# Infini-attention and SwiGLU, two layers on one core: K's masked odd copy on a compute engine, corner masks in halves, and a new hand-written order

## The chip, the cores and the metric

One core of a Trainium2 chip runs the whole program; the metric is its time on the device in microseconds. TensorE multiplies into PSUM, ScalarE and VectorE read PSUM and write SBUF, GpSimd works in SBUF alone, and SyncE issues most of the DMAs. In rows of a profile the engines are PE (PEld: its weight loads), ACT, DVE, POOL and SP.

## The reference

Two layers of the same two blocks over 2048 tokens of width 512. `_A_ref` has 32 heads of width 16 and goes through the sequence in four segments of 512 tokens: softmax attention inside a segment, mixed by a gate with a read of a memory M that the earlier segments have filled. `_B_ref` is a gated feed-forward block of width 1376.

```python
for s in range(N):                                  # 4 segments of L = 512
    logits = jnp.einsum('bhqd,bhkd->bhqk', qs, ks) * scale + mask
    p = _softmax(logits, axis=-1)
    a_dot = jnp.einsum('bhqk,bhkd->bhqd', p, vs)
    ...
    o = g * a_mem + (1.0 - g) * a_dot
    M = M + jnp.einsum('bhld,bhle->bhde', pk, vs)
...
x = x + _A_ref(_layernorm(x, axis=-1), A_wq, A_wk, A_wv, A_wo, A_beta)
x = x + _B_ref(_layernorm(x, axis=-1), B_w1, B_w3, B_w2)   # and both once more
```

The mask is causal: a query sees the keys up to its own place in its segment.

## The kernel before

The work is cut into eight passes g = 0 to 7 (two layers of four segments). A pass has a layer norm, the projections to Q, K and V (`project`), attention in units (`attention`), the memory's update and read, the output projection, a second layer norm and the feed-forward block (`ffn`). Passes overlap: while the attention of g runs, TensorE also has the feed-forward matmuls of g - 1 and the projections of g + 1.

**Attention units.** `unit_list` cuts a pass into units of up to 512 columns for four heads at a time, 18 in a pass (pass 0 runs in two parts). Of each unit TensorE writes the logits (operations R, line 983) into PSUM, ScalarE writes their exponential to a tile `e` (line 999), GpSimd zeroes what the causal mask hides in it (line 1008, `affine_select`), and two units later TensorE multiplies by V (operations C, line 1054). A unit of kind "f" holds blocks of keys by queries, with a mask of 4 x 64 elements a partition for each block on the diagonal. A unit of kind "s" holds the shared corners: 32 blocks of 64 columns, masked by two instructions of 2048 elements a partition, one on 64 partitions and, behind it, one on 128. There are 16 such units.

**K's masked copies.** The heads lie 16 rows apart, and a matmul takes 32 rows. For the heads with an odd number the kernel keeps a copy of K in which the even rows are zero (tile `km`, its "odd" columns, `kodd`), for the corners a second one in which the odd rows are zero ("even" columns, `kev`, operation ke). In passes 0 and 1 the odd copy is a VectorE multiplication of K by a column of zeros and ones (`cm[1]`, line 795). From pass 2 on the zeros already stand in the two buffers of `km`, and four DMAs of 64 KB, on GpSimd's queue, copy only the odd rows of K (line 803): 24 DMAs in all. Logits of odd heads and of corners wait for them.

**The order.** The operations are built in program order, and then issued in an order written out by hand: `ORDER` lists all 3699 operations by number, over all engines at once; each engine takes its own in that order, and buffers are handed out along it. `OTHER` lists the operations that have two possible engines and take the second one: evacuations of PSUM (`ev`, line 519 on VectorE and 518 on ScalarE), ke, and some steps of the normalisation. Waits between engines are semaphores. One rule is added in `schedule`: an operation of GpSimd waits for all VectorE operations of the kinds in `SHARED` that stand ahead of it in the order. Names that the prediction uses: norm (line 689), vj (a shifted copy of V, line 785), phmin (line 832), evv, evk, evq, evt (evacuations of V, K, Q and of the transposed input), macc (line 862, an addition to the memory).

```python
SHARED = ("vj", "ke", "norm", "lnve", "t", "rdg", "ph", "phmin", "mblk", "km", "oadd")
            ...
            if e == "dve" and op.group[0] in SHARED:
                handed.append(op)
            elif e == "pool" and op.dmaq is None:
                for d in handed:
                    op.deps[d.seq] = d
                handed = []
```

Of the kernel before, what the change touches and what calls it, by code (L numbers as in the profile page):

```python
# [3 lines left out]
ACT = mybir.ActivationFunctionType  # L4
# [4 lines left out]
P = 128  # L9
# [3 lines left out]
NCG = 4  # L13
# [239 lines left out]
def o_pe(ns):  # L253
# [7 lines left out]
    0 9 30 23 29 32 2-3 31 34 33 35 5 10 4 21 1 11-12 36-37 13-16 6 17 44 38-39 45-46 18-19 40 47-48 20 41 55 43 22  # L261
    49-53 56 42 57 78-79 102 8 80 90-91 103 92 81 85 68 54 86-88 82 7 67 58-59 69 60 83 104-107 61 108 89 84 27 64
    93-94 109-110 186 188 97-99 113-114 100 115-116 111 95 187 117-118 24 189 119-120 191 112 96 101 200 673 201 70
    121 671 62-63 74-75 667 65 674 66 71 25 127-128 194 196 190 129 672 134-136 668 193 137-138 669-670 675-676
    139-140 154-155 195 208 141-142 130 197-198 224 122 72-73 192 209 199 225 156-157 145 131 146 123-124 147 158
    125 210 365 226 211 215 214 680 159-160 212 165 148 143 677 126 179 166 227 231 149-150 161 213 133 202-204 366
    683 151-152 167-169 162 180 229 153 132 174 368 170 230 256 258 175 181 228 216 369 163 257 686 144 171-172 259
    367 164 173 371 176 264 177 358 217 265 207 178 240 266 182 267 684 241 260 248 261 685 183 274 76 206 269 268
    678-679 275 744 205 272-273 270 218 271 687 745 681 276 249 277 262 184 746 370 284 185 232 688 682 263 1112
    705 242 747 77 285 28 722 282 233 283 250 748 243 280 706-708 281 26 709 1113 251 739-742 294 710 244-245 743  # L270
    278-279 286 689 723 252 254 296 295 724 246 297 300 700 1114-1115 298 253 1108 1110 701 372 219 308 299 287 725
    1109 220 304 1111 1116 309 726 234 305 690 247 702 691-692 703 306 302 704 301 235 373-374 310 1117 1119
    236-237 711 288 238 307 239 320 376 303 1122 328 1118 321 693 712 329 318 713 319 324 716 332 311 694 322 333
    1121 377 695 325-326 714-715 1120 323 378 756 327 1123 696-697 222 698 344 289 334 717 749 255 345 342-343 757
# [146 lines left out]
def build(nc, A_x, A_wq, A_wk, A_wv, A_wo, A_beta, B_w1, B_w3, B_w2, out):  # L421
# [530 lines left out]
    def attention(s, g, z, oms, parts):  # L952
        z.ot = new("W")
        cnt = 0
        for pi, part in enumerate(parts):
# [4 lines left out]
            for ui, (blocks, done, N) in enumerate(todo):  # L960
# [3 lines left out]
                for pgs in groups:  # L964
# [22 lines left out]
                    for (kind, G, ee, j, c, n) in blocks:  # L987
# [6 lines left out]
                        if kind == "s" or ee:  # L994
                            rd += [(z.km, G, j // 2)] if g <= 1 else [(z.km, pg, "p") for pg in pgs]
# [288 lines left out]
```

## Time and profile before

| | us |
|---|---|
| three runs of the kernel before | 495.35, 501.39, 504.0 |
| their median | 501.39 |
| the profiled execution, its own time | 496.81 |
| its span, first to last instruction | 495.1 |

The profile is of one execution, 4.6 us faster than the median of the three runs. Its time is 1.7 us more than its span. Times in rows are from the span's start. A row of the timeline gives start and duration, both in us, the engine, the line, the operation and its tiles; "x8" means that eight instructions in a row are merged into one, under the form of the first, and a bracket names how long the engine stood idle ahead of it and what ended that. PEclk is TensorE's granted clock as a share of 2.4 GHz.

### The profile page before, as it was taken

How to read it: one execution, taken by the hardware profiler on the slowest of the kernel's cores; microseconds unless marked ns; L12 is line 12 of the kernel's file. 1: busy time of each engine (PE TensorE's matmuls, PEld its weight loads, DVE VectorE, ACT ScalarE, POOL GpSimd, SP SyncE). 2: the span in 40 equal slices, each digit the busy share in tenths (PEclk: the TensorE clock that was granted, in tenths of full speed). 3: DMA queues.
4: the chain of work that ended last, by engine and by line, in shares of the span. 5: the costliest groups of instructions: out<-in, count | busy, mean ns of one | idle time of the engine just before them, and what ended most of it. 6: DMA issues, size and time to landing. Idle time of an engine off the chain costs nothing.

```text
span 495.1 us, 19697 instructions
## 1 busy us (share of the span) xinstructions
PE 470.1 (95%) x8808; PEld 241.0 (49%) x8808; DVE 401.2 (81%) x836; ACT 376.4 (76%) x359; POOL 251.2 (51%) x408
## 2 busy tenths in 40 slices
PE   7789989799999998999999999899999999999997
PEld 4444435576445443544444545354444544455554
DVE  7998899588699788788987888886796699689673
ACT  6687997589899997799988879779997887651130
POOL 4774276275538573556745554755474743540000
PEclk9888999799999999999999999999999999999999
DMA  7662427733522725443254613444224411441402
GB/s 242 242 98 50 83 56 138 117 78 71 72 45 56 98 34 97 65 69 68 33 93 57 98 27 66 59 72 87 44 34 72 50 39 28 80 75 54 99 1 77
DMA packets 106548, 37.49 MB, mean 76 GB/s; under 512 B 99200, under 2 KB 104448, under 8 KB 106464
## 3 DMA queue, kind: packets, MB, share of 16 engines
q1 hardware_dynamic: 104016, 31.41, 33.8%
q0 software_dynamic: 1488, 4.03, 5.1%
q8 instruction: 69, 1.13, 1.0%
q10 hardware_dynamic: 960, 0.79, 0.5%
q14 instruction: 15, 0.12, 0.1%
HBM read 8.43 MB, written 2.10 MB: 21 GB/s over the span
## 4 chain that ended last, share of the span: by engine, by line
PE 78%; DVE 12%; DMA 4%; issue 2%; ACT 2%; POOL 1%; SPq 0%; POOLq 0%
PE psall L233 32%; PE psall L228 30%; PE psall L983 8%; PE psall L1054 6%; DVE W L832 2%; DMA W<-xn 2%; ACT e L999 1%; DVE xn L689 1%; DMA x_tok<-in_A_x_dram 1%; DVE W L519 1%; DVE ln L670 1%; DVE km L795 1%; DVE vj L785 1%; POOL e L1008 1%; DMA xg<-xs 1%
## 5 line engine op out<-in xcount | busy, mean ns | idle before, releaser
L999 ACT ACTIVATE e<-psall 128x2048 bf16<-128x2048 f32 (+1 forms) x162 | 271.3, 1691 | 46.3 <-PE psall L983 44.3
L1008 POOL TENSOR_SCALAR_AFFINE_SELECT e<-e 128x256 bf16<-128x256 bf16 (+2 forms) x288 | 173.7, 627 | 135.3 <-ACT e L999 76.0
L228 PE MATMUL psall<-W,w 128*128 128x512 bf16 (+1 forms) x365 | 84.3, 360 | 1.5 <-DMA W<-xn 1.0
L233 PE MATMUL psall<-W,w 128*32 128x512 bf16 (+1 forms) x1420 | 82.2, 361 | 0.0
L1173 ACT ACTIVATE th<-psall 128x512 bf16<-128x512 f32 x80 | 47.1, 600 | 24.2 <-PE psall L233 21.4
L1179 DVE SCALAR_TENSOR_TENSOR h<-gp,psall 128x512 bf16<-128x512 bf16 x80 | 53.7, 679 | 11.8 <-PE psall L228 5.8
L1175 DVE SCALAR_TENSOR_TENSOR gp<-th,psall 128x512 bf16<-128x512 bf16 x80 | 53.8, 680 | 11.2 <-ACT th L1173 10.7
L233 PE MATMUL psall<-w,h 128*32 128x512 bf16 (+2 forms) x968 | 58.0, 370 | 1.3 <-DVE h L1179 1.3
L228 PEld LDWEIGHTS psall<-W,w 128*128 128x128 bf16 x365 | 33.8, 100 | 35.6 <-issue 3.8
L233 PEld LDWEIGHTS psall<-W,w 128*32 128x32 bf16 x1420 | 37.1, 97 | 27.1 <-issue 4.0
L670 DVE BATCH_NORM_STATS2 ln<-x_tok 128x6 f32<-128x512 bf16 x64 | 42.9, 679 | 1.6 <-DMA x_tok<-in_A_x_dram 1.2
L1091 POOL TENSOR_TENSOR og<-xg,rd 128x256 bf16<-128x256 bf16 (+1 forms) x46 | 27.7, 606 | 31.9 <-DVE rd L1085 12.6
L519 DVE CAST W<-psall 128x512 bf16<-128x512 f32 (+1 forms) x48 | 32.0, 677 | 9.8 <-PE psall L228 7.0
L1054 PE MATMUL psall<-e,va 128*32 128x192 bf16 (+4 forms) x1088 | 39.6, 266 | 0.1
L1198 DVE TENSOR_TENSOR x_tok<-psall,x_tok 128x512 bf16<-128x512 f32 (+1 forms) x33 | 22.0, 673 | 21.4 <-PE psall L233 13.1
L983 PE MATMUL psall<-W,km 32*128 32x64 bf16 (+4 forms) x1056 | 37.5, 230 | 0.0
L233 PEld LDWEIGHTS psall<-w,h 128*32 128x32 bf16 (+1 forms) x968 | 25.2, 96 | 21.3 <-issue 2.1
L1054 PE MATMUL psall<-e,vj 128*32 128x64 bf16 x1024 | 30.1, 194 | 4.2 <-issue 3.4
L228 PE MATMUL psall<-wv,W 128*128 128x512 bf16 x94 | 30.0, 397 | 4.0 <-DVE va L519 3.7
L228 PE MATMUL psall<-w,h 128*128 128x512 bf16 (+1 forms) x121 | 32.4, 380 | 0.0
L983 PE MATMUL psall<-W 16*128 16x64 bf16 (+4 forms) x544 | 31.4, 274 | 0.8 <-DVE W L519 0.6
L679 POOL TENSOR_TENSOR ln<-ln,mhalf 128x4 f32<-128x4 f32 (+1 forms) x17 | 16.8, 989 | 29.7 <-DVE ln L676 26.7
(98 smaller groups left out, 671.5 us busy)
## 6 DMA issues: line engine op xcount, KB each, us to landing
w<-in_B_w_dram SPq DMA_DIRECT2D x4, 688.0 KB, 8.5
out_dram<-x_tok SPq DMA_DIRECT2D x15, 128.0 KB, 1.8
km<-W POOLq DMA_DIRECT2D x24, 64.0 KB, 3.4
w<-in_B_w_dram POOLq DMA_DIRECT2D x3, 384.0 KB, 5.2
x_tok<-in_A_x_dram POOLq DMA_DIRECT2D x2, 512.0 KB, 8.8
xg<-xs SPq DMA_TRANSPOSE x36, 3.3
W<-og SPq DMA_TRANSPOSE x36, 2.6
wk<-in_A_wk_dram SPq DMA_DIRECT2D x1, 512.0 KB, 4.5
```

Source lines behind the costliest of these rows:

```text
L228: return e.matmul(out, lhsT, rhs, **k)
L233: o = e.matmul(out[c:c + 32], lhsT[:, c:c + 32], rhs, tile_position=(0, c), **k)
L519: return e.tensor_copy(dst(), src())
L670: dve(lambda e: e.bn_stats(ln_r[st.slot][:, i, 0:6], x_tok[:, tt, :]), 540, reads=[("x", tt)], writes=[(st, 0, i)], bufs=[st], prio=prio, ...
L983: o = e.matmul(S4[:, sps(pg), c:c + n], kk, q_r[z.q.slot][r, G, q0:q0 + n], start=True, stop=True, tile_position=(32 * pg, 0))
L999: act(lambda e, N=N, ebuf=ebuf, pgs=pgs, sps=sps: e.activation(e_r[ebuf.slot][:, pgs[0]:pgs[-1] + 1, 0:N], S4[:, sps(pgs[0]):sps(pgs[-1]) ...
L1008: pool(lambda e: e.affine_select(view(), view(), pattern=pattern, compare_op=ALU.is_ge, fill=0.0, base=base, channel_multiplier=-1), n, re ...
L1054: o = e.matmul(bank(X)[32 * pg:32 * pg + 32, at:at + m], (va_r[z.va.slot] if kind == "f" else vj_r[z.vj.slot])[:, j, h:h + 32], e_r[eb.slo ...
L1091: return e.tensor_tensor(ogv()[:, 0:nt, :, k, :], src, v(1)[:, k, :, :, None].to_broadcast([P, nt, 4, DH]), ALU.mult)
L1173: act(lambda e, NW=NW, B=B, th=th: e.activation(th_r[th.slot][:, 0:NW], bank(B)[:, 0:NW], ACT.Tanh, scale=0.5), NW, reads=[(B, 0)], writes ...
L1175: dve(lambda e, NW=NW, B=B, th=th, gp=gp: e.scalar_tensor_tensor(gp_r[gp.slot][:, 0:NW], th_r[th.slot][:, 0:NW], 1.0, bank(B)[:, 0:NW], AL ...
L1179: dve(lambda e, NW=NW, B=B, gp=gps[fg], h=hs[fg]: e.scalar_tensor_tensor(h_r[h.slot][:, 0:NW], gp_r[gp.slot][:, 0:NW], 0.5, bank(B)[:, 0:N ...
```

## The change

The odd copy of K is made by a compute engine in all eight passes: the 24 DMAs of line 803 go, and 12 multiplications of two column groups each (1024 elements a partition) come in passes 2 to 7. They have two possible engines; by the new `OTHER`, seven of them are on VectorE and five on ScalarE. Each of the two corner masks is cut in two by heads (`a`), so that a corner unit has four masks of 1024 elements in place of two of 2048. All four must be done before V is multiplied. The `km` buffer is now taken at K's projection in every pass. `ORDER` and `OTHER` are written anew, for 3719 operations.

```diff
@@ ORDER, OTHER: all numbers anew @@
-    0 9 30 23 29 32 2-3 31 34 33 35 5 10 4 21 1 11-12 36-37 13-16 6 17 44 38-39 45-46 18-19 40 47-48 20 41 55 43 22
...
@@ project @@
-                       hold=[{"q": z.q, "k": z.k, "v": z.va}[kind]] + ([z.km] if kind == "k" and g <= 1 else []), name="%s%d.%d" % (kind, G, cg))
+                       hold=[{"q": z.q, "k": z.k, "v": z.va}[kind]] + ([z.km] if kind == "k" else []), name="%s%d.%d" % (kind, G, cg))
...
-            if kind == "k" and g <= 1:
-                dve(lambda e, part=part, Gs=Gs, c0=c0, c1=c1: e.tensor_scalar(
...
-            elif kind == "k" and Gs[0] == NCG - 1:
-                for pg in range(4):
-                    r = slice(32 * pg + 16, 32 * pg + 32)
-                    S.add([("pool", 1000.0, 2000.0)], lambda e, r=r: e.dma_start(kodd(km_r[z.km.slot])[r],
-                                                                              k_r[z.k.slot][r].rearrange("p g (j c) -> p g j c", c=P)), dmaq="pool",
...
+            if kind == "k" and (hf is not None or g == 1 or Gs[0] % 2):
+                Gm = Gs if hf is not None or g == 1 else (Gs[0] - 1, Gs[0])
+                mkeys = [(G, h) for G in Gm for h in (range(2) if hf is None else (hf,))]
+
+                def odd(e, Gm=Gm, c0=c0, c1=c1):
+                    dst = kodd(km_r[z.km.slot])[:, Gm[0]:Gm[-1] + 1, c0 // P:c1 // P, :]
+                    src = k_r[z.k.slot][:, Gm[0]:Gm[-1] + 1, c0:c1].rearrange("p g (j c) -> p g j c", c=P)
+                    if hasattr(e, "activation"):
+                        return e.activation(dst, src, ACT.Copy, scale=cm[1][:, 0:1])
+                    return e.tensor_scalar(dst, src, cm[1][:, 0:1], None, op0=ALU.mult)
+                S.add([o_dve(W * len(Gm), False, 1.5), o_act(W * len(Gm), False)], odd, reads=[(z.k,) + x for x in mkeys] + ["cm1"],
+                      writes=[(z.km,) + x for x in mkeys], bufs=[z.k, z.km], prio=p0 + 0.02 - (100 if g == 0 else 0), name="km")
@@ attention @@
-                            rd += [(z.km, G, j // 2)] if g <= 1 else [(z.km, pg, "p") for pg in pgs]
+                            rd.append((z.km, G, j // 2))
...
-                    for h in range(2):
-                        cut(("s", h), 64 * h, rd=rd + [(ebuf, "s", 0)] * h, view=lambda ebuf=ebuf, h=h: e_r[ebuf.slot][0:64 * h + 64, :, :].rearrange(
-                            "p g (b c) -> p (g b) c", c=64), pattern=[[0, 32], [1, 64]], n=2048)
+                    for a in range(2):
+                        for h in range(2):
+                            cut(("s", a, h), 64 * h, rd=rd + [(ebuf, "s", a, 0)] * h, view=lambda ebuf=ebuf, h=h, a=a: e_r[ebuf.slot][
+                                0:64 * h + 64, 2 * a:2 * a + 2, :].rearrange("p g (b c) -> p (g b) c", c=64), pattern=[[0, 16], [1, 64]], n=1024)
```

The new order moves instructions on every engine. Three places follow. The first is VectorE in pass 0, between the first evacuations of V and the second layer norm's input. Before (xn is norm, va is evv, vj the shifted copy, W from psall an evacuation of K or Q):

```order
L519 CAST va<-psall 128x16x2x16
L689 TENSOR_SCALAR xn<-x_tok,ln 128x512
L795 TENSOR_SCALAR km<-W,cm 128x2x2x128
L689 TENSOR_SCALAR xn<-x_tok,ln 128x512
L519 CAST va<-psall 128x16x2x16
L785 COPY vj<-va 64x2x320
```

After, at the same place of VectorE:

```order
L521 CAST va<-psall 128x16x2x16 x2
L521 CAST W<-psall 128x2x256 x2
L787 COPY vj<-va 64x2x320
L678 TENSOR_SCALAR ln<-ln 128x4
L831 TENSOR_SCALAR W<-W 128x1024
L805 TENSOR_SCALAR km<-W,cm 128x2x2x128
L831 TENSOR_SCALAR W<-W 128x1024
L787 COPY vj<-va 64x2x320
L521 CAST va<-psall 128x16x2x16
L691 TENSOR_SCALAR xn<-x_tok,ln 128x512 x3
```

The second evacuation of V stood behind two norms and a km; now it stands right behind the first, and norm and km come later.

The second place is VectorE at the end of pass 0's attention, where the transposed input of pass 1 is evacuated (COPY W from psall is evt). Before:

```order
L785 COPY vj<-va 64x2x320
L832 TENSOR_TENSOR W<-W,px 128x1024
L785 COPY vj<-va 64x2x320
L519 COPY W<-psall 128x512 x2
L670 BN_STATS ln<-x_tok 128x6
```

After:

```order
L787 COPY vj<-va 64x2x320 x2
L521 CAST xs<-psall 128x512
L521 COPY W<-psall 128x512
L672 BN_STATS ln<-x_tok 128x6
L521 COPY W<-psall 128x512
L672 BN_STATS ln<-x_tok 128x6
L521 COPY W<-psall 128x512
L521 CAST xs<-psall 128x512
```

A vj stood directly ahead of the last two evt; now both vj are done before the evacuations begin.

The third place is GpSimd in the middle of pass 1's attention, with the late loads of weights and input on its queue. Before:

```order
L509 DMA w<-in_B_w_dram 128x512
L803 DMA km<-W 16x16x128
L509 DMA w<-in_B_w_dram 128x3x512
L803 DMA km<-W 16x16x128
L509 DMA w<-in_B_w_dram 128x3x512
L509 DMA x_tok<-in_A_x_dram 128x4x512
L1008 AFFINE_SELECT e<-e 128x4x64 x4
L803 DMA km<-W 16x16x128
L1008 AFFINE_SELECT e<-e 128x4x64 x2
L803 DMA km<-W 16x16x128
```

After:

```order
L511 DMA w<-in_B_w_dram 128x512
L1009 AFFINE_SELECT e<-e 128x4x64 x2
L511 DMA w<-in_B_w_dram 128x3x512
L1009 AFFINE_SELECT e<-e 128x4x64 x5
L511 DMA w<-in_B_w_dram 128x3x512
L511 DMA x_tok<-in_A_x_dram 128x4x512
L1009 AFFINE_SELECT e<-e 128x4x64 x3
```

The four km DMAs are gone, and masks stand between the loads of weights, but the last of these and the load of the input still follow each other directly.

## Rows read from the trace of the kernel before

**Rows 1.** The page: busy time by engine, TensorE in 40 slices (tenths).
```profile
PE 470.1 (95%) x8808; PEld 241.0 (49%) x8808; DVE 401.2 (81%) x836; ACT 376.4 (76%) x359; POOL 251.2 (51%) x408
...
PE   7789989799999998999999999899999999999997
```

**Rows 2.** TensorE's waits: waiting and releasing line, us in total, times, longest.
```profile
PE psall L228 <- DVE va L519: 4.1, 2, 3.7
PE psall L1054 <- issue: 3.4, 1, 3.4
...
PE psall L228 <- DVE macc L862: 1.6, 1, 1.6
```

**Rows 3.** Windows: stretch, its length, busy by engine, granted clock, DMA share, GB/s.
```profile
18.90:22.90 4.00, 0.30 (x4) 0.03 (x2) 3.97 (x5) 1.65 (x2) 4.00 (x7) 0.81 0.29 95
22.90:28.00 5.10, 5.10 (x33) 2.27 (x37) 4.58 (x11) 2.27 (x3) 2.76 (x6) 0.50 0.00 0
...
34.90:39.00 4.10, 1.82 (x54) 0.78 (x52) 4.07 (x7) 1.55 (x2) 4.03 (x4) 0.93 0.74 98
39.00:41.60 2.60, 2.60 (x11) 0.89 (x7) 1.88 (x8) 1.94 (x2) 0.28 (x2) 0.50 0.03 6
...
89.50:93.20 3.70, 0.29 (x20) 0.18 (x16) 1.60 (x5) 0.51 (x2) 0.71 (x1) 0.98 0.89 154
93.20:99.90 6.70, 6.70 (x86) 4.13 (x87) 2.43 (x7) 3.82 (x4) 1.42 (x3) 0.50 0.27 57
```

**Rows 4.** Timeline of VectorE, 16.9 to 23.4 us.
```profile
17.13 2.13 DVE L689 TENSOR_SCALAR xn<-x_tok,ln 128x512 bf16<-128x512 bf16 x1
19.18 2.63 DVE L795 TENSOR_SCALAR km<-W,cm 128x512 bf16<-128x512 bf16 x1
```

**Rows 5.** Timeline of GpSimd, the same stretch.
```profile
17.00 6.66 POOL L1008 TENSOR_SCALAR_AFFINE_SELECT e<-e 64x2048 bf16<-64x2048 bf16 x8
```

**Rows 6.** GpSimd's groups by form: count, busy us, mean ns, idle before.
```profile
L1008 POOL TENSOR_SCALAR_AFFINE_SELECT e<-e 128x256 bf16<-128x256 bf16 x256 | 107.0, 441 | 119.0 <-ACT e L999 66.1 <-DVE xn L689 11.0 <-DVE W L832 9.4
...
L1008 POOL TENSOR_SCALAR_AFFINE_SELECT e<-e 128x2048 bf16<-128x2048 bf16 x16 | 33.8, 2115 | 1.0 <-DVE og L1091 0.5
```

**Rows 7.** Timeline, 34.4 to 39.2 us.
```profile
34.58 4.30 POOL L1008 TENSOR_SCALAR_AFFINE_SELECT e<-e 64x2048 bf16<-64x2048 bf16 x2 [0.87 <-ACT e L999]
...
34.60 2.27 DVE L785 COPY vj<-va 64x640 bf16<-64x640 bf16 x1
...
37.71 0.40 PE L233 MATMUL psall<-W,wk 128*32 128x512 bf16 x4 [2.28 <-DVE W L519]
```

**Rows 8.** Timeline at 69.4 us, and at 230.3 us.
```profile
69.61 3.21 DVE L832 TENSOR_TENSOR W<-W,px 128x1024 bf16<-128x1024 bf16 x1
...
230.44 1.88 DVE L785 COPY vj<-va 64x1280 bf16<-64x1280 bf16 x1
```

**Rows 9.** VectorE lines: min/median/max ns of one; the last by form, mean ns.
```profile
L795 DVE TENSOR_SCALAR km<-W,cm x9: 269/344/2627, 8.9 to 66.2; 128x512 bf16<-128x512 bf16 x7, 128x256 bf16<-128x256 bf16 x2
L785 DVE COPY vj<-va x18: 309/487/2266, 22.8 to 395.6; 64x1280 bf16<-64x1280 bf16 x14, 64x640 bf16<-64x640 bf16 x4
L832 DVE TENSOR_TENSOR W<-W,px x24: 657/681/3820, 27.9 to 362.3; 128x1024 bf16<-128x1024 bf16 x24
L817 DVE TENSOR_SCALAR km<-W,cm 128x1024 bf16<-128x1024 bf16 x5 | 2.4, 478 | 0.0
```

**Rows 10.** Timeline of ScalarE at 378 us, and the window around it.
```profile
378.00 1.14 ACT L816 ACTIVATE km<-W,cm 128x1024 bf16<-128x1024 bf16 x1
376.00:381.00 5.00, 5.00 (x112) 2.40 (x105) 2.53 (x7) 3.46 (x3) 2.97 (x8) 1.00 0.70 120
```

**Rows 11.** DMA queues, 80 to 93.2 us: packets, MB, share of 16 engines.
```profile
q0 software_dynamic: 465, 1.51, 59.6%
...
q8 instruction: 2, 0.03, 1.6%
```

**Rows 12.** The same, 166 to 172 us, where q0 holds four km DMAs alone.
```profile
q0 software_dynamic: 128, 0.26, 39.0%
```

More of the change, by code (lines that the diff above doesn't have):

```diff
@@ L266 @@
[L266 to L270, printed above, removed]
@@ new lines @@
+    1163-1164 783 1148 386 1165 1149 780 342-343 367 759 77 387 1150 785 1185 388 897 389 1186 1151 784 1187 899
+    390-391 903 1188 393 392 395 1166 786 1175 795 344 396 345 394 1189 787 1158 766 1159-1160 767-768 1167 789
+    1176-1177 1161 796 1162 908 771 791 1197 909 1180-1181 790 1178 772 1190 1182 1191 1183 792 1192-1193 1198
+    397-398 357-361 1179 1337 801 1137 1199 400 1153 399 788 793 1138-1139 401 1154 1194 797 1184 1155 802
+    1156-1157 775 1140 366 776 1338 1141 799 905-906 805 794 773 769 800 407-408 798 402 774 806 770 403 809 421
@@ new lines @@
+    2067-2068 2416-2417 2441-2442 1457 2069 2072 2055 2065 1458 2443 2073 2070-2071 2423 1459 2444-2445 1444 2424
+    2184 2446-2447 1749 2425-2426 1765 2434 1766 1460 2448 2076 2435 2427 1461 2436-2437 2077 2428 2478 2078 2187
+    2429 2438 2430-2432 2466 2418-2419 2449-2450 2079 2467 2451 2471 2452 2481 2468 2453 2479 2082 2482 1691 2483
+    2083 2469 2472 2470 1768 1748 2480 1767 1769 2420 1478 2473-2475 2080 2086 1479 2074 1750 2075 2421 2081
+    1462-1463 2085 1480-1481 1751 2087 2422 1482 2056 1464-1465 2456 2084 2484 2457 1466 2618 2616 2485 1483
@@ L1019, in attention @@
                 if sh:
-                    for h in range(2):
-                        cut(("s", h), 64 * h, rd=rd + [(ebuf, "s", 0)] * h, view=lambda ebuf=ebuf, h=h: e_r[ebuf.slot][0:64 * h + 64, :, :].rearrange(
-                            "p g (b c) -> p (g b) c", c=64), pattern=[[0, 32], [1, 64]], n=2048)
+                    for a in range(2):
+                        for h in range(2):
+                            cut(("s", a, h), 64 * h, rd=rd + [(ebuf, "s", a, 0)] * h, view=lambda ebuf=ebuf, h=h, a=a: e_r[ebuf.slot][
+                                0:64 * h + 64, 2 * a:2 * a + 2, :].rearrange("p g (b c) -> p (g b) c", c=64), pattern=[[0, 16], [1, 64]], n=1024)
                 for b in sh:
-                    where[("s", b[1], b[3])] = (ebuf, b[4], 64, [(ebuf, "s", h) for h in range(2)])
+                    where[("s", b[1], b[3])] = (ebuf, b[4], 64, [(ebuf, "s", a, h) for a in range(2) for h in range(2)])
                 waiting += [(ui + C_LAG, G, how, pr) for (G, how) in done]
```

287 lines of the change are left out of this document (139 added, 148 removed), and 15 rows, old and new, of the table OTHER.

## The prediction

> **What bounds the kernel now.** I read the page first. TensorE is busy 95% of the span, VectorE 81%, ScalarE 76% [rows 1]. Its slices show where the missing 5% lies: after the first third nearly every slice is full, the gaps are in the first 100 us and in the tail. So no engine beside TensorE has to get faster on average; what counts is each place at which TensorE stands still, and what its clock does behind that.
>
> The list of TensorE's waits names three places [rows 2]. All waits together are 25.0 us (the span of 495.1 less the 470.1 busy), and these places, with one of 2.28 us at 37.7 us [rows 7], hold 11.4 us of it, nearly half. The windows around them show the second half of the price: after a wait of a few microseconds the granted clock is 0.50, the lower of its two levels, for 5.1 us, 2.6 us and 6.7 us [rows 3]. At half clock half of such a stretch is lost, though TensorE counts as busy in it.
>
> Then I ask who made them wait. At 22.9 us TensorE waits for an evacuation of V on VectorE. VectorE is not short of speed there: a norm takes 2.13 us and a km 2.63 us [rows 4], where the median km takes 0.34 us [rows 9]. Beside them GpSimd runs eight masks without a break, 6.66 us [rows 5], the two corner masks of 2.1 us each among them [rows 6]. The norm ends when the first corner mask ends, and the km when the second does. At 34.6 us the same thing befalls a vj: 2.27 us beside two corner masks, where the shortest takes 0.31; the evacuation behind it is late, and TensorE waits 2.28 us [rows 7, 9]. At 69.6 us it is a phmin of 3.21 us, with a median of 0.68, and the wait for macc follows [rows 2, 8, 9]. So some VectorE instructions and GpSimd's masks exclude each other, and the long masks are the long waits. The last large wait is of another kind: at 89.5 us TensorE stops in the middle of an operation, and no semaphore released it ("issue", 3.4 us, [rows 2, 3]), while the DMA engines are loaded to the full by late loads of weights and input, four km DMAs and transposes; instruction packets are on the same engines [rows 11].
>
> **The change, part by part.** The sum is made against the profiled execution's own 496.8 us.
>
> *First place, 18.9 to 28.0 us.* In the new order the evacuations of V stand ahead of norm and km on VectorE. Of the 3.7 us of waiting I leave 0.3, and of the 5.1 us at half clock nothing: 3.4 + 2.55 = 6.0 us gained. Bounds: 2 us, if another evacuation is 2 us late in its place and the clock falls all the same, and 6.25 us.
>
> *Second place, 34.9 to 41.6 us.* Both vj now stand ahead of the evacuations that gate TensorE. With a vj of median 0.49 us in place of 2.27 [rows 7, 9] the wait shrinks by 1.8 us, and the 2.6 us at half clock lose their 1.3: 3.1 us. Bounds: 1.8, if the clock falls anyway, and 3.6 us.
>
> *Third place, 69.6 us.* A phmin held by a corner mask has a surplus of 2.5 us; held by a half it loses about half of that, 1.2 us, and the wait for macc shrinks as much. Bounds: 0 and the whole 1.6.
>
> *Corner masks in halves.* From 441 ns for 256 elements and 2115 for 2048 [rows 6], a mask of 1024 is an estimate of 1.14 us. 64 of these are 73.0 us, 32 of before are 67.7: GpSimd has 5.3 us more, on an engine that is 51% busy, and the chain in front of a corner's multiplication with V grows by 0.3 us in 16 units, which have two units of time to be masked. I take no cost for that; without that cover it is 16 x 0.3 = 5 us. What the halves bring depends on the order. The km at 19.18 us began 0.3 us ahead of the second corner mask, yet had to wait for its end as well: as long as GpSimd has masks standing, they pass VectorE by [rows 4, 5]. The rule of `SHARED`, by which a mask waits for VectorE operations ahead of it in the order, lets VectorE in; the halves give it more places for that. What stretches of the smaller size cost is shown by a vj: the one at 230.4 us (1.88 us against 0.49) ended no wait of the size of those listed [rows 2, 8, 9]. The Trainium skill ("SBUF — State Buffer", Who interferes with whom) has an exclusive lock on the port pair, held for one whole instruction. By that alone each half would set VectorE free after 1.1 us, wherever it stands in the order, and the remaining stretches would shrink by half for certain; the trace's km, held across two masks, does not bear that out, and I stay with the row. For the later stretches (the longest is a phmin of 3.82 us [rows 9]) I take 1 us, between -2 (a loss) and 3.
>
> *The km DMAs.* No wait of TensorE's list is for a km DMA [rows 2], so their latency is worth nothing. Their load is: from 80 to 93.2 us GpSimd's queue holds 59.6% of 16 engines, 7.9 us [rows 11], and four km DMAs by themselves took 39.0% of 6 us, 2.3 us, for 0.26 MB [rows 12]. The backlog in which TensorE stops so gets shorter by 2.3 us of 7.9. The stop and its half clock cost 3.4 + 3.35 = 6.8 us. If the stop ends with the backlog, 2.3 of it go; with a shorter stop I count a third of the clock's loss as saved: 3.5 us. Bounds: 0, since the last load of weights and that of the input still follow each other directly in GpSimd's order, and 6.8.
>
> *The copies in their place.* Twelve of 1024 elements. On VectorE the nearest row is the ke of 1024, 478 ns [rows 9]: seven are 3.4 us. On ScalarE the ke takes 1.14 us [rows 10]: five are 5.7 us. What hides them is slack: around the ke at 378 us TensorE is busy in all of 5.00 us at full clock [rows 10]. They also take GpSimd's port on VectorE, and the new order as a whole will have new near misses. I charge 2 us, between 0 and the full 9.1.
>
> The sum: -6.0 - 3.1 - 1.2 - 1.0 - 3.5 + 2.0 = -12.8, so **484.0 us** on the profiled execution's scale. The median of three runs lies 4.6 us above that execution, and what the slower runs had in addition is not shown; if stops like that at 89.5 us vary between runs, the lighter queue takes part of it away. I add half, 2.3 us: **486 us**, 3% under 501.39.
>
> **The rivals.**
> *The stretches move.* In the new order, too, VectorE operations of these kinds stand behind masks, in passes 4 and 6 a vj behind two halves. If halves without a gap hold VectorE as the whole masks did, two waits like those at 22.9 and 34.9 us come back elsewhere in about their old size, 6.0 + 3.1 us: 486 + 9 = 495 us, no change that can be told. For it: the km held across two masks [rows 4, 5]. Against it: both places with the highest price are reordered, and late in the program TensorE has work beside the waits [rows 1].
> *The stop stays whole.* The late loads meet the same part of TensorE's program, the stop and its half clock remain, and only the 3.5 us for it are not gained: 489.5 us. The Trainium skill ("Runtime: NRT & Kernel Launch", Instruction fetch mechanics) says that fetching the next instructions is mostly hidden; by that the stop is not a fetch that competes with the loads, and taking km DMAs away would leave it alone, which is this case.
> *ScalarE and VectorE become the bound.* An exponential paces each unit, and a copy of 1.14 us ahead of it delays it in full if ScalarE has no idle time there. If all twelve copies come through to TensorE, 9.1 us, and each wait is followed by 1.3 us lost to the half clock as at 39.0 us (15.6 us), that is 24.7 - 2.0 already charged, on 486: 509 us, slower than before. It decides from the point where ScalarE's idle time between exponentials is under a copy's 1.14 us in most of the passes. Against it: the ke at 378 us, and 24% of ScalarE idle [rows 1, 10].
> *The change as named does nothing:* the copy was on no path. The time would then hang on the order alone, which is the first rival's case.
>
> **How the numbers follow.** The forecast has 0.45, the stop that stays 0.18, the moved stretches 0.27, the bound on ScalarE and VectorE 0.10. A measurement of this kernel can tell about 2% from no change, 10 us: faster is under 491.4, slower over 511.4. The forecast and the whole stop lie below that, but the stop only just, so a quarter of its chance goes to no change: faster 0.45 + 0.13 = 0.58. No change has 0.27 + 0.05 and half of the slower case, whose 509 us lie just inside: 0.37. Slower keeps 0.05. The range reaches down to 477: the stop gained whole (3.3 us more), the copies free (2.0), the later stretches at 3 us (2.0) and most of the 2.3 us that I added for the median. It reaches up to 500: the moved stretches, with 5 us more for the copies.
>
> **What would show it.** In the profile after: no wait for an evacuation over 1 us before 45 us, and a clock of 1.00 there; no norm, km, vj or phmin on VectorE over 1.6 us; masks of 1024 near 1.14 us, copies near 0.48 and 1.14 us; GpSimd's queue with 24 DMAs less; the stop near 90 us shorter than 3.4 us. I am wrong if TensorE's waits still add up to 25 us, if stretches of VectorE sit beside pairs of halves and gate TensorE, or if exponentials are late behind copies.

## The result and the profile after

| | us |
|---|---|
| kernel before, median of 4 runs (lowest, highest) | 499.25 (495.35, 504.0) |
| kernel after, median of 4 runs (lowest, highest) | 477.35 (474.29, 477.75) |
| ratio after to before, 95% interval | 0.9573 [0.9484, 0.9662] |
| profiled execution after, its time and its span | 477.68, 475.9 |

The kernel is 4.3% faster, where the forecast was 3%. Later comparisons have their own runs of before (medians 497.45, 498.4 and 498.1 us), so times from different ones are compared by their ratios. A ratio leaves out executions that were slow as a whole: one of the four of before (504.0 us), and two of the ten of the halves alone, the profiled one among them, so that only durations and the order of events are read from its trace.

The page after, busy time and TensorE's slices and clock, answers to [rows 1]:

```profile
PE 461.8 (97%) x8757; PEld 237.7 (50%) x8793; DVE 388.8 (82%) x843; ACT 380.9 (80%) x362; POOL 242.3 (51%) x418
...
PE   8989989999999999999999999999999999999997
...
PEclk9979999999999999999999999999999999999999
```

The span is 19.2 us shorter. TensorE's idle time is 475.9 - 461.8 = 14.1 us in place of 25.0, which is 10.9 us of it; the other 8.3 are less busy time. The mean granted clock over the span rose from 0.983 to 0.993, which by estimate makes some 5 us of that (1.7% of 495.1 less 0.7% of 475.9). One slice of PEclk is still low, the third. TensorE's waits after, to be held against [rows 2]:

```profile
PE psall L228 <- issue: 2.1, 13, 0.2
PE psall L984 <- issue: 1.3, 1, 1.3
PE psall L550 <- DVE xs L547: 1.3, 1, 1.3
PE psall L984 <- ACT e L1000: 1.1, 1, 1.1
PE psall L701 <- DVE W L521: 0.6, 1, 0.6
```

The three places of [rows 2] are gone from the list, and so is the wait of 2.28 us of [rows 7]. The windows say what the clock did, the first two and the last two over the stretches of [rows 3]:

```profile
18.90:22.90 4.00, 3.88 (x88) 2.36 (x86) 3.94 (x11) 4.00 (x5) 3.67 (x7) 1.00 0.34 111
22.90:28.00 5.10, 4.53 (x121) 2.90 (x122) 5.10 (x10) 4.91 (x8) 3.69 (x9) 1.00 0.51 129
30.00:37.00 7.00, 6.56 (x61) 2.44 (x63) 5.83 (x17) 3.84 (x5) 5.40 (x7) 0.53 0.38 75
...
89.50:93.20 3.70, 3.24 (x112) 2.41 (x109) 3.51 (x8) 3.43 (x4) 3.08 (x6) 1.00 0.63 125
93.20:99.90 6.70, 6.70 (x143) 5.02 (x141) 6.20 (x16) 6.26 (x6) 5.64 (x8) 1.00 0.32 63
```

The first place and the stretch near 90 us run at full clock now. But a stretch at the lower level, 1.2 GHz, stands at 30 to 37 us, where before had none. Three short waits of TensorE precede it (the timeline, where each bracket is a wait):

```profile
27.08 0.21 PE L1056 MATMUL psall<-e,vj 128*32 128x64 bf16 x4 [0.35 <-DVE xs L521]
28.54 0.40 PE L701 MATMUL psall<-ident,xn 128*128 128x128 bf16 x4 [0.60 <-DVE W L521]
30.39 0.61 PE L984 MATMUL psall<-W,km 32*128 32x256 bf16 x4 [1.11 <-ACT e L1000]
```

The steps named in advance, by VectorE's and ScalarE's lines (min/median/max ns) and GpSimd's corner masks by form:

```profile
L833 DVE TENSOR_TENSOR W<-W,px x24: 659/686/1389, 25.0 to 345.4; 128x1024 bf16<-128x1024 bf16 x24
L787 DVE COPY vj<-va x18: 307/480/543, 20.6 to 372.7; 64x1280 bf16<-64x1280 bf16 x14, 64x640 bf16<-64x640 bf16 x4
L691 DVE TENSOR_SCALAR xn<-x_tok,ln x64: 314/408/1220, 5.2 to 441.2; 128x512 bf16<-128x512 bf16 x64
L804 ACT ACTIVATE km<-W,cm x6: 752/1140/1197, 17.8 to 312.0; 128x1024 bf16<-128x1024 bf16 x5, 128x512 bf16<-128x512 bf16 x1
```

```profile
L1009 POOL TENSOR_SCALAR_AFFINE_SELECT e<-e 128x1024 bf16<-128x1024 bf16 x32 | 36.8, 1155 | 1.8 <-DVE rd L1087 0.5 <-DVE xn L691 0.4 <-DVE og L1098 0.3
L1009 POOL TENSOR_SCALAR_AFFINE_SELECT e<-e 64x1024 bf16<-64x1024 bf16 x32 | 36.1, 1139 | 15.8 <-ACT e L1000 12.6 <-DVE om L901 1.3 <-DVE W L831 0.7
```

The longest phmin (L833) went from 3.82 to 1.39 us, the longest vj (L787) from 2.27 to 0.54, the longest norm (L691) is 1.22 [rows 4, 9]. A half takes 1.14 to 1.16 us, as estimated. On VectorE a copy of 1024 elements takes 0.55 us on average, where 0.48 were forecast; on ScalarE it takes 1.15, where 1.14 were. GpSimd's queue has 720 packets in place of 1488.

Where the 19.2 us came in is seen by the start of the same exponential in both traces. Exponentials are numbered from 0 within a pass, in program order (pass 0 has 36, the others 18):

| exponential | before | after | gained so far |
|---|---|---|---|
| pass 0, no. 12 | 31.7 | 26.7 | 5.0 |
| pass 0, no. 33 | 52.3 | 49.0 | 3.3 |
| pass 1, no. 3 | 72.4 | 68.9 | 3.5 |
| pass 1, no. 9 | 94.1 | 84.6 | 9.5 |
| pass 2, no. 3 | 129.7 | 115.6 | 14.1 |
| pass 3, no. 3 | 177.8 | 163.8 | 14.0 |
| pass 3, no. 9 | 197.2 | 181.0 | 16.2 |
| pass 6, no. 3 | 340.2 | 322.7 | 17.5 |
| end of the span | 495.1 | 475.9 | 19.2 |

The head gives 5 us and takes 1.7 back, pass 1 gives over 10, passes 3 to 6 the rest. The experiments ask why.

### The profile page after: what moved, and what is told of

Same layout as the page of the kernel before. It is cut to its first block, busy times and chain, and to the rows that moved or that the text cites. A ratio compares the mean times of both kernels' runs of the same rounds, so it can differ in the third digit from the quotient of the medians.

```text
span 475.9 us, 19641 instructions
## 1 busy us (share of the span) xinstructions
PE 461.8 (97%) x8757; PEld 237.7 (50%) x8793; DVE 388.8 (82%) x843; ACT 380.9 (80%) x362; POOL 242.3 (51%) x418
## 3 DMA queue, kind: packets, MB, share of 16 engines
q8 instruction: 69, 1.13, 1.0%
## 4 chain that ended last, share of the span: by engine, by line
PE 85%; DVE 9%; ACT 3%; issue 1%; DMA 1%; POOL 0%; DVEq 0%; POOLq 0%
PE psall L228 34%; PE psall L233 33%; PE psall L984 9%; PE psall L1056 7%; ACT e L1000 2%; DVE W L521 1%; DVE xn L691 1%; DVE va L521 1%; DVE W L831 1%; DVE W L833 1%; DVE ln L672 1%; DMA x_tok<-in_A_x_dram 1%; PE psall L856 0%; DVE vj L787 0%; DVE xs L521 0%
## 5 line engine op out<-in xcount | busy, mean ns | idle before, releaser
L233 PE MATMUL psall<-W,w 128*32 128x512 bf16 (+1 forms) x1352 | 79.0, 361 | 0.0
L233 PE MATMUL psall<-w,h 128*32 128x512 bf16 (+3 forms) x916 | 54.7, 370 | 0.0
L233 PEld LDWEIGHTS psall<-W,w 128*32 128x32 bf16 x1352 | 33.7, 97 | 25.8 <-issue 1.7
L521 DVE CAST W<-psall 128x512 bf16<-128x512 f32 (+1 forms) x44 | 29.5, 674 | 8.8 <-PE psall L228 4.8
L1200 DVE TENSOR_TENSOR x_tok<-psall,x_tok 128x512 bf16<-128x512 f32 (+1 forms) x33 | 21.5, 669 | 17.5 <-PE psall L233 13.3
L1093 POOL TENSOR_TENSOR og<-xg,rd 128x256 bf16<-128x256 bf16 (+1 forms) x43 | 25.6, 600 | 18.2 <-DVE rd L1087 6.2
L228 PE MATMUL psall<-w,h 128*128 128x512 bf16 (+1 forms) x124 | 31.4, 379 | 1.4 <-issue 1.1
L233 PEld LDWEIGHTS psall<-w,h 128*32 128x32 bf16 (+1 forms) x916 | 23.1, 96 | 18.5 <-issue 2.5
L691 DVE TENSOR_SCALAR xn<-x_tok,ln 128x512 bf16<-128x512 bf16 x64 | 26.8, 455 | 5.1 <-POOL ln L681 5.1
L984 PEld LDWEIGHTS psall<-W,km 32*128 32x128 bf16 x1056 | 15.9, 93 | 29.4 <-ACT e L1000 17.0
```

What stands on the lines that cost most here:

```text
L228: return e.matmul(out, lhsT, rhs, **k)
L233: o = e.matmul(out[c:c + 32], lhsT[:, c:c + 32], rhs, tile_position=(0, c), **k)
L521: return e.tensor_copy(dst(), src())
L691: op = S.add([o_dve(512, False, 1.45)], lambda e, i=i, k=k, tt=tt, xn=xn: e.tensor_scalar(xn_r[xn.slot][:, k, :], x_tok[:, tt, :], ln_r[st ...
L984: o = e.matmul(S4[:, sps(pg), c:c + n], kk, q_r[z.q.slot][r, G, q0:q0 + n], start=True, stop=True, tile_position=(32 * pg, 0))
```

## The experiments

**The parts on the new order.** Three kernels have the new order. In the first the masks are whole and the km DMAs are back, so that the order alone is new; the second has whole masks only; the third has the DMAs only.

```diff
-                    for a in range(2):
-                        for h in range(2):
-                            cut(("s", a, h), 64 * h, ... n=1024)
+                    for h in range(2):
+                        cut(("s", h), 64 * h, ... n=2048)
```

```diff
-            if kind == "k" and (hf is not None or g == 1 or Gs[0] % 2):
+            if kind == "k" and g in (2, 3, 4, 5, 6, 7):
+                if Gs[0] == NCG - 1:
+                    for pg in range(4):
+                        S.add(... e.dma_start(kodd(km_r[z.km.slot])[r], ...) ... dmaq="pool", name="km")
+            elif kind == "k" and (hf is not None or g == 1 or Gs[0] % 2):
```

> The new order alone: whole corner masks again (each at the place of its first half) and the 24 km DMAs again (each behind the TensorE operation that stood ahead of it before, and not before its K is there). My theory, three parts that add up: the order takes the stretched VectorE instructions out of TensorE's way, the missing km DMAs end the stop near 89 us, the halves add little. Then the stop with its half clock (6.8 us) and part of the stretches are back: 485 to 490 us. Rival, the order is everything: 477 us. Rival, the copies and halves are everything: 497 us.

Measured: 483.53 us, ratio 0.9716 [0.9662, 0.977]. That is below the 485 to 490 expected, and far from both rivals.

> The changed kernel with whole corner masks, each at the place of its first half; copies and order stay. My theory: the new order has few VectorE operations of the blocked kinds directly behind corner masks, so a stretch of up to 2 us appears in some places and gates TensorE in one or two: 478 to 483 us. Rival, the halves are what ended the long stretches: VectorE is held 2 us at ten places again and the time is above 487 us.

Measured: 479.68 us, ratio 0.9632 [0.9583, 0.9681], as expected.

> The changed kernel with the 24 km DMAs of passes 2 to 7 in place of the twelve copies; halves and order stay. My theory: the load of four more DMAs in the late loads brings back the stop of TensorE between 78 and 95 us with a half clock behind it, 3 to 7 us, and the other 20 DMAs cost nothing: 480 to 485 us. Rival, the stop went because of the order of the late loads, not because of the km DMAs: 477 us and no stop over 1.5 us.

Measured: 481.67 us, ratio 0.969 [0.9629, 0.975]. The time is as expected, but the stop that was to make it did not come.

The order alone makes two thirds of the gain, 2.8 of 4.3%. With it the copies bring 0.8% (0.9716 to 0.9632) to 1.2% (0.969 to 0.9573), the halves 0.3 to 0.6%, less than their intervals can tell. With whole masks the longest phmin is already short, so it is the place beside the masks that shortens it, not their size. The norms are another matter: with the order alone one takes 2.28 us beside whole masks, and TensorE waits 1.00 us for the step of the feed-forward block (h) that stands behind it; with whole masks and copies it is 2.18 and 0.86 us. In the new kernel no norm is over 1.22 us and this wait is gone. So the size of the masks counts there. Order alone, VectorE's lines and TensorE's wait:

```profile
L840 DVE TENSOR_TENSOR W<-W,px x24: 657/686/1385, 25.0 to 351.0; 128x1024 bf16<-128x1024 bf16 x24
L690 DVE TENSOR_SCALAR xn<-x_tok,ln x64: 314/409/2277, 5.2 to 447.0; 128x512 bf16<-128x512 bf16 x64
```

```profile
306.80 0.62 PE L233 MATMUL psall<-w,h 128*32 128x512 bf16 x8 [1.00 <-DVE h L1187]
```

And the stop near 90 us does not come back with the km DMAs, nor its half clock. The kernel before from 80 to 88 us, and then the third kernel, where the DMA engines are about as full (1.16 for 1.19):

```profile
80.00:88.00 8.00, 7.04 (x203) 4.86 (x203) 7.42 (x16) 7.25 (x8) 6.56 (x13) 1.00 1.19 198
```

```profile
80.00:88.00 8.00, 7.71 (x225) 6.01 (x221) 7.27 (x19) 8.00 (x9) 6.67 (x13) 1.00 1.16 196
88.00:100.00 12.00, 10.81 (x309) 8.11 (x297) 10.81 (x24) 10.54 (x11) 9.46 (x13) 1.00 0.64 89
```

So the km DMAs, whose load was the prediction's reason for the stop, need not go for it to end.

The km DMAs cost something elsewhere. In the third kernel VectorE stands 1.47 us for a transpose that took 5.9 us to land while a km DMA was under way, and TensorE waits 1.31 us for the feed-forward step (gp) that VectorE does two instructions later. With the order alone the same wait is 1.26 us. The two kernels with copies have no wait there, and in the new kernel the transposes at this point take 3.2 us. VectorE's row and TensorE's in the third kernel:

```profile
208.93 0.35 DVE L1094 RECIPROCAL rd<-xg 128x32 f32<-128x32 bf16 x1 [1.47 <-DMA xg<-xs]
```

```profile
210.17 1.05 PE L233 MATMUL psall<-W,w 128*32 128x512 bf16 x16 [1.31 <-DVE gp L1186]
```

**The two VectorE places alone.** The kernel before, with two pieces of VectorE's order changed:

```diff
-L519 CAST va<-psall 128x16x2x16
+L519 CAST va<-psall 128x16x2x16 x2
 L689 TENSOR_SCALAR xn<-x_tok,ln 128x512
 L795 TENSOR_SCALAR km<-W,cm 128x2x2x128
 L689 TENSOR_SCALAR xn<-x_tok,ln 128x512
-L519 CAST va<-psall 128x16x2x16
...
+L519 COPY W<-psall 128x512 x2
 L785 COPY vj<-va 64x2x320
-L519 COPY W<-psall 128x512 x2
```

> The kernel before with two places of VectorE's order changed and nothing else: the second evacuation of V ahead of norm and km near 19 us, and two evacuations of the transposed input ahead of a vj near 35 us. My theory: both waits of TensorE shrink to under 1 us and the half clock behind them goes, 9 us less than the kernel before: 488 us on the scale of 497. Rival, the wait only moves: the held VectorE instructions then gate the next operation of TensorE, and the time is 494 to 499 us.

Measured: 494.82 us, ratio 0.9956 [0.9914, 0.9998], the rival's time. Its TensorE timeline:

```profile
23.70 0.61 PE L228 MATMUL psall<-wv,W 128*128 128x512 bf16 x1 [3.35 <-DVE W L519]
...
37.73 0.81 PE L228 MATMUL psall<-wv,W 128*128 128x512 bf16 x3 [0.97 <-DVE xs L519]
```

The second place's wait shrank from 2.28 to 0.97 us. The first only moved: TensorE now waits 3.35 us for the next evacuation, which stands behind the same km (2.63 us again, beside the same masks), and the window 23.7 to 31.0 us has a clock of 0.60. So at the first place the rival of the moved stretches is right, as far as one other place for the evacuation was tried and GpSimd's masks stood where they were. The second place's half clock is gone, though, and at exponential no. 33 of pass 0 this trace (492.46 us, the fastest of its ten) is 3.6 us ahead of before, where the new kernel is 3.3 us ahead.

**The copies alone, the halves alone, the late loads alone.** Each is the kernel before in its own order with one thing changed. For the copies, the DMAs of line 803 are replaced as in the change's diff. For the halves:

```diff
-                    for h in range(2):
-                        cut(("s", h), 64 * h, ... n=2048)
+                    for a in range(2):
+                        for h in range(2):
+                            cut(("s", a, h), 64 * h, ... n=1024)
```

For the loads, GpSimd's order:

```diff
 L509 DMA w<-in_B_w_dram 128x3x512
 L803 DMA km<-W 16x16x128
+L1008 AFFINE_SELECT e<-e 128x4x64 x4
+L803 DMA km<-W 16x16x128
+L509 DMA x_tok<-in_A_x_dram 128x4x512
+L1008 AFFINE_SELECT e<-e 128x4x64 x2
 L509 DMA w<-in_B_w_dram 128x3x512
-L509 DMA x_tok<-in_A_x_dram 128x4x512
-L1008 AFFINE_SELECT e<-e 128x4x64 x4
-L803 DMA km<-W 16x16x128
-L1008 AFFINE_SELECT e<-e 128x4x64 x2
```

> The kernel before in its own order and with whole masks of the shared corners; only the 24 km DMAs are replaced by the twelve copies on VectorE and ScalarE, each at the place where the new kernel has it relative to TensorE's work. Nothing of the computation is left out. Theory of the prediction (the load of the km DMAs makes TensorE's stop near 89 us): the stop of 3.4 us is under 1 us, no half clock behind it, and 3.5 to 6.8 us less, 490.5 to 494 on the scale of 497.4, less a little for the copies. Rival (the stop hangs on where the late loads of weights and input meet TensorE's program, which this kernel does not change): a stop of about 3 us stays, and the time is 496 to 499. The copies by themselves should cost no more than 2 us in either case.

Measured: 496.31 us, ratio 0.995 [0.9918, 0.9983]. The time is the rival's; the trace below fits neither reading whole.

> The kernel before in its own order and with its km DMAs; only each corner mask of 2048 is two of 1024, one directly behind the other. Nothing of the computation is left out. Reading of the row (GpSimd's masks that stand in a row pass VectorE by): norm, km, vj and phmin beside them still take 2 to 3.8 us, the waits of 3.7, 2.3 and 1.6 us stay within 0.5 us of their size, and the time is 496 to 500. Reading of the lock (each half sets VectorE free when it ends): these operations take at most about 1.6 us, the three waits shrink by about half, 3 to 4 us, with some of the half clock behind them, and the time is 490 to 494.

Measured: 501.84 us, ratio 1.0045 [1.0002, 1.0087], above what either reading expected.

> The kernel before with its km DMAs and whole masks; only the late loads of weights and the last load of the input are moved on GpSimd's queue to the places that they have in the new kernel relative to TensorE's work, so that masks and a km DMA stand between them. Nothing of the computation is left out. Theory now (the run of loads that stands together on the queue makes the stop): no stop of over 1 us near 89 us, no half clock behind it, and 5 to 7 us less, 490 to 492 on the scale of 497.4. Theory of the prediction (the load of the km DMAs): the stop stays at about 3 us and the time at 496 to 498. A third reading (the stop comes when a fetch of TensorE's instructions falls into a full DMA queue, whatever fills it): it may come at another place, and the longest instruction packet between 75 and 100 us then takes over 2 us beside it.

Measured: 491.0 us, ratio 0.9864 [0.9799, 0.9928], as the theory of the run of loads expected.

The late loads alone, a move of two instructions on a queue, bring 7.4 us of medians, a third of the whole change. In its trace 7.0 us come in pass 1 (2.0 earlier at exponential no. 3, 9.0 at no. 15); the 2.0 us ahead of that lie before the first moved load and are not the change's. No stop and no half clock are left there, though all four km DMAs are there and the DMA engines are nearly as full (1.10):

```profile
80.00:88.00 8.00, 7.57 (x187) 5.64 (x181) 7.69 (x19) 7.23 (x9) 4.91 (x11) 1.00 1.10 176
88.00:100.00 12.00, 10.95 (x313) 8.85 (x312) 10.70 (x23) 10.65 (x11) 9.60 (x12) 1.00 0.73 160
```

The copies alone end the "issue" stop too, but a wait for a transposed tile takes its place, with a half clock behind it. TensorE with the copies alone, timeline and window:

```profile
85.73 0.38 PE L228 MATMUL psall<-W,w 128*128 128x256 bf16 x2 [2.66 <-DMA W<-xn]
```

```profile
86.00:90.00 4.00, 3.95 (x38) 2.57 (x40) 2.01 (x5) 1.57 (x3) 0.68 (x2) 0.57 0.66 153
```

So with the loads in a row less traffic gives time back, about as much as the prediction had it, but in another way: the stop went whole and a wait for a transpose came. Exponential no. 3 of pass 2 comes 3.1 us earlier (forecast 3.5), and of that 2.2 is left at the end.

The halves alone are no gain. In the head they do what the lock says: beside twelve masks without a break the km takes 1.29 us in place of 2.63 and the norms 1.05 and 1.59. The first two of the three waits shrink (2.38 us for 3.70, 1.31 for 2.28), the clock is 1.00 from 16 to 32 us, and the exponential no. 33 of pass 0 comes 4.2 us earlier. The Trainium skill's lock, held for one whole instruction ("SBUF — State Buffer", Who interferes with whom), agrees there. In pass 5 it does not: a phmin takes 3.94 us beside five masks without a break, two of them halves. The wait for macc does not shrink either (1.78 us for 1.62). The masks of pass 5, and VectorE's lines:

```profile
321.19 3.33 POOL L1016 TENSOR_SCALAR_AFFINE_SELECT e<-e 128x1024 bf16<-128x1024 bf16 x5
```

```profile
L840 DVE TENSOR_TENSOR W<-W,px x24: 657/681/3937, 26.5 to 367.4; 128x1024 bf16<-128x1024 bf16 x24
L812 DVE TENSOR_SCALAR km<-W,cm x9: 267/347/1289, 9.4 to 62.0; 128x512 bf16<-128x512 bf16 x7, 128x256 bf16<-128x256 bf16 x2
```

Both readings are right in places; no run shows what decides between them. And in this trace the 4.2 us are lost again in pass 1, by one wait of 4.37 us for a transpose and a stop of 3.71; the ten executions lie between 495.39 and 504.21 us, this one at 504.03, and of the others there is no trace. From 76.6 to 91.6 us two transposes take 14.4 and 15.5 us to land, and no instruction packet (queue q8) arrives:

```profile
q1 hardware_dynamic: 2339, 0.58, 57.6%
q0 software_dynamic: 459, 1.49, 54.2%
issues: line engine op xcount, KB each, median us to landing
x_tok<-in_A_x_dram POOLq DMA_DIRECT2D x1, 512.0 KB, 13.5
...
xg<-xs SPq DMA_TRANSPOSE x1, 14.4
W<-W SPq DMA_TRANSPOSE x1, 15.5
```

**The loads together in the new kernel.** The same question from the other side: the new kernel, which has no km DMAs, with only the loads' places changed. The unchanged new kernel ran beside it.

```diff
 L511 DMA w<-in_B_w_dram 128x512
+L1009 AFFINE_SELECT e<-e 128x4x64 x5
+L511 DMA w<-in_B_w_dram 128x3x512 x2
+L511 DMA x_tok<-in_A_x_dram 128x4x512
...
-L511 DMA w<-in_B_w_dram 128x3x512
-L1009 AFFINE_SELECT e<-e 128x4x64 x5
-L511 DMA w<-in_B_w_dram 128x3x512
-L511 DMA x_tok<-in_A_x_dram 128x4x512
```

> The new kernel once more, unchanged, so that the next two can be compared with it on one chip: 474 to 478 us, about 0.957 of the kernel before. Every theory expects the same of it.

Measured: 477.16 us (476.06 to 477.71, 6 runs), ratio 0.9572 [0.9531, 0.9613].

> The new kernel with its copies and halves; only the late loads of weights and the last load of the input stand together on GpSimd's queue again, at the places that they have in the kernel before relative to TensorE's work. Nothing of the computation is left out. Theory (the run of loads that stands together delays transposes and instruction packets; where it is spread, nothing waits): a wait of 1 to 4 us for a transpose or for issue comes back between 75 and 95 us, and the time is 2 to 5 us over the new kernel's, 478 to 482. Theory of the prediction (the km DMAs fill the queue): without them the loads may stand together, no wait of over 1 us there, and the time is within 1 us of the new kernel's.

Measured: 482.64 us (477.85 to 483.59, 6 runs), ratio 0.9666 [0.9619, 0.9713], 5.5 us over the new kernel beside it and just above the 478 to 482 expected. The stop is back without a single km DMA, at another instruction (L233) but nearly the same time, and the half clock behind it:

```profile
86.97 1.15 PE L233 MATMUL psall<-W,w 128*32 128x256 bf16 x34
91.18 0.61 PE L233 MATMUL psall<-W,w 128*32 128x256 bf16 x14 [3.06 <-issue]
```

```profile
88.10:91.20 3.10, 0.04 (x6) 0.02 (x5) 0.00 (x0) 0.61 (x2) 2.05 (x4) 1.00 1.26 141
91.20:98.00 6.80, 5.86 (x151) 3.57 (x151) 5.46 (x10) 3.60 (x4) 2.61 (x3) 0.59 0.95 140
```

The queues from 79.6 to 88.6 us, just into the stop, with the loads together, and then in the new kernel:

```profile
q0 software_dynamic: 334, 1.24, 78.3%
q1 hardware_dynamic: 1094, 0.27, 24.8%
```

```profile
q0 software_dynamic: 256, 0.92, 33.1%
q1 hardware_dynamic: 2341, 0.58, 32.3%
q8 instruction: 1, 0.02, 0.8%
```

With the loads together GpSimd's queue holds 78.3% of the engines, the transposes' queue (q1) moves half as much (0.27 MB for 0.58), and q8, the instruction packets, is not there at all. TensorE stops in the middle of a run of equal matmuls (34 done, 14 to come).

**A phmin later.** The three short waits ahead of 30 us stand behind a VectorE that is busy 6.94 of 7.00 us from 24 to 31. In it is a phmin of 1.39 us whose result goes to a DMA that TensorE does not wait for there. It is moved behind the four evacuations (COPY W) that TensorE does wait for, and one evacuation of finished units (CAST xs) behind the first of these:

```diff
-L833 TENSOR_TENSOR W<-W,px 128x1024
-L521 CAST xs<-psall 128x512
 L818 TENSOR_SCALAR km<-W,cm 128x2x2x64 x2
 L691 TENSOR_SCALAR xn<-x_tok,ln 128x512
 L521 COPY W<-psall 128x512
+L521 CAST xs<-psall 128x512
...
+L833 TENSOR_TENSOR W<-W,px 128x1024
```

> The new kernel, but on VectorE the first phmin of pass 0's attention (1.39 us at 25.0 us, beside masks) stands behind the four evacuations of the transposed input of pass 1, its transfer behind it, and one evacuation of the finished units stands behind the first of the four. Nothing of the computation is left out. Theory (VectorE is full from 20 to 31 us, and what nobody waits for stands ahead of what TensorE waits for): the waits at 27.1, 28.5 and 30.4 us, 2.06 us together, shrink to under 0.7, the half clock from 30 to 37 us (about 3.3 us lost) goes or gets shorter, and the time is 1.5 to 4.5 us under that of the new kernel, 472 to 475 where that has 476 to 477. Rival (the wait only moves, as with the two places alone): another wait of over 1 us before 45 us takes their place, the half clock stays, and the time is within 1 us of the new kernel's.

Measured: 475.0 us (474.8 to 475.09), ratio 0.9536 [0.9489, 0.9583], at the upper end of what was expected.

> The kernel with the first phmin of pass 0 behind the four evacuations of the transposed input of pass 1, beside the new kernel on one chip. Nothing of the computation is left out. If the half clock at 30 to 37 us comes from the waits ahead of it, this kernel shows clock 1.00 in every run and stays at 475 us within 0.5 us, while the new kernel is 1 to 2.5 us higher and spreads over 3 us, with its clock under 1.00 in the slower runs. If the half clock had been chance, both kernels have the same median within 0.7 us.

Measured: 475.33 us (474.37 to 475.67, 6 runs) against 477.16 (476.06 to 477.71) of the new kernel beside it; ratio to before 0.9538 [0.9501, 0.9575]. The two ranges do not touch. Of this version's ten runs eight have a granted clock of 1.00 over the whole span, two 0.996, where all were expected to keep it; the six of the new kernel beside it have 0.993 or 0.996. The new kernel's first four runs have 0.993, 0.999, 0.993 and 0.996, and the one of 0.999 took 474.29 us, the least of its ten: the same order can keep the clock, and its time is then that of the later phmin. The same window with the phmin later:

```profile
30.00:37.00 7.00, 6.47 (x136) 3.26 (x136) 6.90 (x21) 6.04 (x8) 5.30 (x7) 1.00 0.39 77
```

Two waits are left ahead of it (0.55 and 0.70 us, 1.25 together for 2.06; under 0.7 was expected). With 0.8 us less waiting the clock stayed up, and the medians differ by 1.8 us. GpSimd gets on earlier too: by `SHARED` it waits for the phmin and the km behind it, and its mask at 27.61 us starts at 26.43 here. The run does not separate this from the evacuations' new place. This version is faster than the new kernel and than the kernel before.

## Why the prediction came out as it did

The forecast was 486 us, the range 477 to 500; 477.35 lies at its lower edge. The sign and the kind of gain were right, but most of the terms were mis-sized, and it is luck that they offset each other: the head was put 5.8 us too high, the stop and the later stretches each over 3 us too low, and the copies were charged as a cost where they gained.

*First and second place: 9.1 us forecast, about 3.3 measured* (exponential no. 33 of pass 0). Both waits went, and no wait for an evacuation over 1 us is left before 45 us. The step that failed is the one on the clock, that "of the 5.1 us at half clock nothing" would be left: a new stretch of nearly 7 us at half clock came 7 us later, behind waits of 0.35, 0.60 and 1.11 us. The later phmin shows the price: with it exponential no. 33 starts at 46.1 us in place of 49.0, so 2.9 of the missing 5.8 us are this stretch and its waits. The other 2.9 are the sizes of the two terms: in that trace the first place gives 4.9 us (exponential no. 12) for the 6.0 forecast, the second 1.3 for 3.1. With the two places moved by themselves the first wait only moved, so there the masks' new places count, as the first rival said. One reading of rows was loose: the vj at 34.60 us was held by the first of its two corner masks alone (36.69 us its end, 36.87 that of the vj).

*Third place: 1.2 us forecast.* The wait for macc is gone whole, the upper bound of 1.6; a wait of 1.34 us of the kind "issue" stands at 68.6 us now.

*The stop: 3.5 us forecast for the km DMAs.* As the effect of the DMAs in the old order the term's size is right (3.1 us with the copies alone), though the way was another. But in the new order the stop of 3.4 us and its half clock of 3.35 went whole, and not for that reason: they go with the loads spread and the DMAs kept, and come back with the loads together and the DMAs gone. The prediction saw that masks stand between the loads now, but used it as a bound only ("the last load of weights and that of the input still follow each other directly"); two of the loads directly in a row did no harm in the new kernel, three within some 2 us did in both. The second rival, the stop that stays, falls. The rule beside it, that fetching is mostly hidden (the Trainium skill, "Runtime: NRT & Kernel Launch", Instruction fetch mechanics), does not hold here: with the loads together no instruction packet came for 9 us ahead of the stop. A gap of that length by itself is not the sign (the new kernel has one from 28.4 to 38.9 us without a stop); that the stop ends with a packet is shown by the last section. The runs on the loads' places show that the packet is late where the loads stand in a row, though none changes the packets alone.

*Later stretches: 1.0 us forecast, between -2 and 3; about 5 measured* (14.0 gained at the start of pass 3, 19.2 at the end). This is not the order's work alone: by the same two points the order alone gains 1.7 us, with the copies 3.2, with the halves 3.8. The trace of before shows waits that the prediction had passed over: 0.74 and 1.20 us in pass 3 (the second of the kind "issue"), and in pass 5 two phmin of 4.63 us together beside four masks, with a step of the feed-forward block (h) behind them, for which TensorE waits. The first row is VectorE's of before, the second TensorE's:

```profile
315.64 4.63 DVE L832 TENSOR_TENSOR W<-W,px 128x1024 bf16<-128x1024 bf16 x2
```

```profile
320.92 1.92 PE L233 MATMUL psall<-w,h 128*32 128x512 bf16 x32 [1.29 <-DVE h L1179]
```

*Halves: no cost taken.* Right, and GpSimd is even busy 8.9 us less (242.3 for 251.2), where the prediction had 5.3 us more: it left out that the issues of the 24 km DMAs took GpSimd 14.2 us. The halves' gain is nothing that the times can tell (0.3 to 0.6% on the new order, a loss of 0.45% on the old); on the new order the traces show it in the norms.

*Copies and near misses: 2.0 us charged.* In the old order the copies lost 0.9 us from pass 2 to the end (3.1 to 2.2); in the new one the DMAs in their place are slower by 1.2%. The step that failed is that the DMAs are worth nothing outside the stop because no wait of TensorE's list is for one: they delay a transpose, that delays VectorE, and TensorE's list names VectorE (1.31 us, near 209 us). No run shows where the rest of the 1.2% lies. The rival in which ScalarE becomes the bound falls: it is busy 80%, and TensorE's longest wait for an exponential is 1.1 us.

*The 2.3 us for the median* rest on no term that a run shows. The new kernel's four runs spread over 3.5 us in place of 8.7, and its median lies at its profiled execution. The later runs of before, 11 to 19 at a time, have medians of 497.45 to 498.4 us, so most of the 4.6 us between the profiled execution and the median was the draw of three runs.

## What to carry to other kernels

Ask of every load that nobody waits for where it stands on its queue: three large ones in a row left transposes 14 us in flight in one trace, went with a late instruction packet and cost 5 to 7 us; with a few masks between them they cost nothing that showed. A wait is not to be counted by its length alone: behind waits of 0.35, 0.60 and 1.11 us came a stretch at half clock, behind 0.55 and 0.70 none. A list of waits names the last one in the chain, so a DMA can cost time without standing in it. And an engine's list of longest instructions is worth reading for the whole program before a term for "the rest" is set.

## What the runs showed of the hardware

TensorE can stop with no semaphore in play until a part of its program has come. In the thirteen traces it does so 34 times for 0.45 us or more ("issue"). 32 of these stops end 1.2 to 1.6 us after an instruction packet of q8 has landed, the other two (the halves alone, the two places) 2.2 and 2.9 us after one. In the kernel before, the stops that end at 71.40, 93.12 and 104.69 us stand after 2241, 3009 and 3521 instructions of TensorE's in the trace, which is 3 x 256 and 2 x 256 apart; the new kernel has 69 such packets, 1.13 MB, for 17,550 matmuls and weight loads, 254 for each. The long stops came with loads in a row: 3.41 us in the kernel before, 3.17 with the two places, 3.71 with the halves alone, 3.06 with the loads together in the new kernel.

```profile
q8 instruction: 69, 1.13, 1.0%
```

A DMA share of 1.10 to 1.16 over 8 us did not do this where the loads were spread, so the share alone does not decide it. And VectorE's instructions beside GpSimd's masks come in two kinds: a km of 1.29 us was through after about one half, a phmin of 3.94 us waited for five masks.
